# RWKV attention and a two-level expert layer on one core: expert inputs as blocks of 32 tokens by 96 values, transposed by VectorE

## The chip, the cores and the metric

The kernel runs on one core of a Trainium2 chip. All data are 32-bit floats. The metric is the device time of one execution in microseconds (us), as the median of several runs. The profile is one further execution, taken by the hardware profiler. The engines are named as the profile names them: PE is TensorE (matrix multiply), PEld its weight load, DVE is VectorE, ACT is ScalarE, POOL is GpSimd, SP is SyncE, which here only starts transfers. A "q" behind an engine's name is its queue of instructions. Lnnn is a line of the kernel before.

## What is computed

An attention block with a state per head comes first, then a mixture of experts whose expert is chosen in two levels.

```python
B, H, S, D = 4, 8, 768, 48
for t in range(S):
    cur = einsum('bhd,bhe->bhde', u * k[:, :, t], v[:, :, t])
    y[:, :, t] = einsum('bhd,bhde->bhe', r[:, :, t], state + cur)
    state = w[..., None] * state + einsum('bhd,bhe->bhde', k[:, :, t], v[:, :, t])
x = y.transpose(0, 2, 1, 3).reshape(3072, 384)
# N, DM, G, Eg, F = 3072, 384, 4, 4, 1024
g_idx = argmax(x @ w_group);          g_w = softmax(x @ w_group)[g_idx]
e_idx = argmax(x @ w_expert[g_idx]);  e_w = softmax(x @ w_expert[g_idx])[e_idx]
out = g_w * e_w * (relu(x @ w1[g_idx, e_idx]) @ w2[g_idx, e_idx])
```

The term with u (the "own term" of a token) needs only r, k, v of that token: the sum over a head of r u k, times v.

## The kernel before

The attention is computed in 24 tiles of 128 tokens (six pieces of the sequence for each of four batches). A loop of 29 steps works as a pipeline: in step s, tile s is turned (`turn`), tile s-1 is scored, tile s-2 is multiplied with v (`values`), tile s-3 is turned back and its own term is added (`back`), and tiles s-4 and s-5 are routed. Two tiles make a pair, and one pair of r, k, v is one load each. The routed rows of 384 values, with two more for the token number and the gate, are scattered to `x_sorted` in DRAM, by expert. Their places are first filled with zeros there, because a fixed number of slots of each expert is processed, filled or not.

```python
SLOTS = [256, 240, 233, 222, 216, 212, 206, 202, 199, 196, 193, 190, 187, 184, 178, 173]
CAP = max(SLOTS); FOUR = 4
w1f = moe_w1.rearrange("g e (ko p) f -> (g e) p ko f", p=P)
...
nothing = cst([P, XW], "nothing")
...
def zero_places(j):
    regions = xs_dram.rearrange("(e n) w -> n e w", e=GE)
    part = CAP // 4
    nc.scalar.dma_start(out=regions[part * j : part * (j + 1)], in_=spread(nothing[0:part, :], 1, GE))
...
def load_expert(e, i, queue=nc.sync):
    w1, w2 = places[i]
    queue.dma_start(out=w1, in_=w1f[bass.ds(e, 1)].rearrange("a p k f -> (a p) k f"))
    queue.dma_start(out=w2, in_=w2f[bass.ds(e, 1)].rearrange("a p k f -> (a p) k f"))
    return w1, w2
...
ITEMS = [(0, 0, P), (0, P, SLOTS[0])] + [(e, 0, SLOTS[e]) for e in range(1, GE)]

def load_rows(i, expert, queue):                       # L472
    ...
    for j, n in enumerate(parts(i)):
        a = ITEMS[i][1] + P * j
        queue.dma_start(out=xg[0:n, j, :], in_=by_expert[bass.ds(expert, 1), a : a + n, :]...)

def columns(i):
    ...
    for ks in (range(0, KO),) if KO * w <= 512 else (range(0, 2), range(2, KO)):
        px = bank([P, len(ks), w], "px")
        for q, ko in enumerate(ks):
            for j, n in enumerate(parts(i)):
                nc.tensor.transpose(px[:, q, P * j : P * j + n],                # L483
                                    xg[0:n, j, P * ko : P * (ko + 1)], ident[0:n, 0:n])
        nc.vector.tensor_copy(xe[:, ks[0] : ks[-1] + 1, 0:w], px)               # L486
    ...                                                # ids and gates from the two last values of xg

def up(i, f): ...      # L506: w1 times xe into ph; ScalarE: relu into hT
def down(i, d): ...    # L520: w2 times hT into po; ScalarE copies to yo
def rows_out(i): ...   # L530: three transposes a part; VectorE times the gate; scatter to out
...
def own(g):            # GpSimd: dg = r * k * u of pair g
def own_sum(g):        # VectorE: du = sum of dg over a head        (L558)
def own_values(n):     # ScalarE: dv = v * du, one product a head   (L564)
...
for s in range(NT + LAST):
    if s % 2 == 0 and s // 2 + 2 < NP: load_pair(s // 2 + 2)
    if s in (3, 5, 7, 9): zero_places(s // 2 - 1)
    if s == FOUR * B + 7:
        first = expert_of(first_i[0:1, 0:1], (SP,))
        weights[0] = load_expert(first, 0)
    if s == FOUR * B + 9:
        load_rows(0, first, nc.sync)
        second = expert_of(first_i[0:1, 1:2], (SP,))
        weights[1] = load_expert(second, 1)
    if s == FOUR * B + 10: columns(0)
    run("first")
    if s < NT: turn(s); ...                            # and own(s // 2 + 1) in odd steps
    for n in range(NT):
        if s == max(n + 1, 2): own_values(n)
    run("choice")
    ...                                                # rows_T, row_logits, back, values
    if s % 2 == 0 and 0 < s // 2 < NP: own_sum(s // 2)
    run("last")                                        # gates, places, scatters of rows
    if 0 <= s - 1 < NT: scores(s - 1)
    ...
    if s == FOUR * B + 10: up(0, 0)
up(0, 2); up(0, 4); ...; up(0, 6)
load_rows(1, first, nc.sync)
...
down(0, 0); ...; down(0, 1); down(0, 2); rows_out(0)
load_rows(2, second, nc.sync)
columns(1)
for i in range(1, len(ITEMS)):                         # this order is kept on TensorE alone
    up(i, 0); up(i, 2)
    if i > 1: rows_out(i - 1)
    up(i, 4); up(i, 6)
    load_rows(i + 2, expert, nc.sync)
    down(i, 0)
    if i + 1 < len(ITEMS): columns(i + 1)
    down(i, 1); down(i, 2)
    weights[e] = load_expert(expert, e % 2)            # the expert of item i + 2
```

The first 16 tiles decide which two experts come first (`pick_first`), so that item 0, the first 128 slots of the first expert, can be computed while the last tiles are still routed. Two sets of weights are held at a time.

Of the kernel before, what the change touches and what calls it, by code (L numbers as in the profile page):

```python
# [8 lines left out]
FP32 = mybir.dt.float32  # L9
# [6 lines left out]
P = 128  # L16
# [18 lines left out]
def kernel(  # L35
# [40 lines left out]
    w1f = moe_w1.rearrange("g e (ko p) f -> (g e) p ko f", p=P)  # L76
# [12 lines left out]
    def cst(shape, name, dtype=FP32):  # L89
        return const.tile(shape, dtype, name=name)  # L90
# [80 lines left out]
    nothing = cst([P, XW], "nothing")  # L171
# [148 lines left out]

    def zero_places(j):

        regions = xs_dram.rearrange("(e n) w -> n e w", e=GE)
        part = CAP // 4
        nc.scalar.dma_start(out=regions[part * j : part * (j + 1)], in_=spread(nothing[0:part, :], 1, GE))
# [101 lines left out]
    def load_expert(e, i, queue=nc.sync):  # L427

        w1, w2 = places[i]
        queue.dma_start(out=w1, in_=w1f[bass.ds(e, 1)].rearrange("a p k f -> (a p) k f"))  # L430
        queue.dma_start(out=w2, in_=w2f[bass.ds(e, 1)].rearrange("a p k f -> (a p) k f"))
        return w1, w2

    def transposed(x, dst):

        px = bank([P, KO, P], "px")
        for ko in range(KO):
            nc.tensor.transpose(px[:, ko, :], x[:, P * ko : P * (ko + 1)], ident)
        nc.scalar.copy(dst, px)
# [7 lines left out]
    by_expert = xs_dram.rearrange("(e n) w -> e n w", e=GE)  # L447
# [14 lines left out]

    def load_rows(i, expert, queue):
        shape = [P, room(i) // P, XW]
        if i < 3:
            xg = pools[0].tile(shape, FP32, name=f"xg_{i}")
        else:
            xg = pools[1].tile(shape, FP32, tag="xg", bufs=3, name="xg")
        xgs[i] = xg
        for j, n in enumerate(parts(i)):  # L470
            a = ITEMS[i][1] + P * j
            queue.dma_start(  # L472
                out=xg[0:n, j, :], in_=by_expert[bass.ds(expert, 1), a : a + n, :].rearrange("a n w -> (a n) w")
            )

    def columns(i):
        xg, w = xgs.pop(i), width(i)
        xe = xes[i] = item_tile(i, [P, KO, room(i)], "xe")
        for ks in (range(0, KO),) if KO * w <= 512 else (range(0, 2), range(2, KO)):
            px = bank([P, len(ks), w], "px")  # L480
            for q, ko in enumerate(ks):
                for j, n in enumerate(parts(i)):
                    nc.tensor.transpose(  # L483
                        px[:, q, P * j : P * j + n], xg[0:n, j, P * ko : P * (ko + 1)], ident[0:n, 0:n]
                    )
            nc.vector.tensor_copy(xe[:, ks[0] : ks[-1] + 1, 0:w], px)  # L486
        ids = item_tile(i, [P, 2], "ids", U32, bufs=4)
        gates = item_tile(i, [P, 2], "gates", bufs=4)
        for j, n in enumerate(parts(i)):
            nc.vector.tensor_scalar(  # L490
                out=ids[0:n, j : j + 1], in0=xg[0:n, j, DM + ROW_ID : DM + ROW_ID + 1], scalar1=float(N),
                scalar2=None, op0=OP.add,
            )
            nc.vector.tensor_copy(gates[0:n, j : j + 1], xg[0:n, j, DM + ROW_GATE : DM + ROW_GATE + 1])
        keys_of[i] = ids, gates
# [155 lines left out]
    def rows_T(n):  # L651
        xTs[n] = pool.tile([P, KO, P], FP32, tag="xT", bufs=2, name="xT")
        c, b = tiles[n]
        transposed(xts[c][:, b, 0:DM], xTs[n])
# [36 lines left out]
    for s in range(NT + LAST):  # L691
# [15 lines left out]
        if s == FOUR * B + 7:  # L707
            first = expert_of(first_i[0:1, 0:1], (SP,))
            weights[0] = load_expert(first, 0)
        if s == FOUR * B + 9:  # L710
            load_rows(0, first, nc.sync)
            second = expert_of(first_i[0:1, 1:2], (SP,))
            weights[1] = load_expert(second, 1)
# [9 lines left out]
        for n in range(NT):  # L723
            if s == max(n + 1, 2):
                own_values(n)
# [10 lines left out]
        if s % 2 == 0 and 0 < s // 2 < NP:  # L736
            own_sum(s // 2)
        run("last")
        if 0 <= s - 1 < NT:
            scores(s - 1)  # L740
        if s == 1:
            own_sum(0)

# [9 lines left out]
        if n in ROUTED:  # L753
# [8 lines left out]
            else:  # L762
                todo.setdefault(s + 1, []).append(("choice", choice))
                todo.setdefault(s + 2, []).extend([("first", before), ("last", gate), ("last", place)])
                for i in range(T):
                    at = s + 3 + (i // 2 if n == FOUR * B - 1 else i)
                    todo.setdefault(at, []).append(("last", lambda i=i, rows=rows: rows(i)))
# [62 lines left out]
    with tc.If(more > 0, preferred_fallthrough_block=False):  # L830
        with tc.tile_pool(name="rest", bufs=1) as rest:
# [15 lines left out]
            with tc.If(ok < 1):  # L847
                with tc.tile_pool(name="scan", bufs=1) as sc:
# [54 lines left out]
                    with tc.For_i(0, NT, 1) as i:  # L903
# [6 lines left out]
                        transposed(xr[:, 0, 0:DM], xT)  # L910
# [62 lines left out]
            with tc.For_i(0, GE, 1) as i:  # L973
                at = nc.values_load(
                    ends_i[0:1, bass.ds(i, 1)], min_val=0, max_val=GE * RG - P,
                    skip_runtime_bounds_check_because="a region holds all tokens and a slot",
                )
                nc.sync.dma_start(out=xs_dram[bass.ds(at, P), :], in_=nothing)
# [4 lines left out]
            with tc.For_i(0, slots, 1) as i:  # L983
# [14 lines left out]
                )  # L998
                xe = tl([P, KO, P], "xe")
                transposed(xg[:, 0:DM], xe)  # L1000
# [50 lines left out]
```

## Time and profile before

| | |
|---|---|
| median of 3 runs | 480.44 us (475.02 to 482.15) |
| the profiled run, its span | 479.58 us, 477.9 us |
| mean granted clock of TensorE | 0.973 of full |
| busy: PE, PEld, DVE, ACT, POOL | 449.7, 430.6, 159.5, 139.0, 129.5 us |
| data moved by DMA | 86.24 MB in 112024 packets, 79633 of them under 512 B |
| transposes of expert inputs on TensorE (L483) | 96, from 168.1 to 447.5 us |
| copies of them by VectorE (L486) | 32, mean 475 ns |
| weights per expert, w1 and w2 | 1536 KB each, 6.8 to 7.1 us from issue to landing |

A line of a timeline gives the start in us, the duration, the engine, the line and operation, output and inputs with their sizes, and in brackets how long the engine had been idle before it and what released it. "[2.88 <-ACT yT L616]" is: idle for 2.88 us, until ScalarE had written yT in line 616. Matmuls are pipelined, so the time that a group of them holds TensorE is read from one start to the next group's start, not from the durations. A 32-bit product is recorded as two instructions.

### The profile page before, as it was taken

The page shows a single profiled execution, that of the slowest core. Times are in us where ns is not written, and L with a number is a line of the kernel's source. Part 1 is how long each engine was busy: PE and PEld are TensorE (multiplying, and loading weights), DVE is VectorE, ACT ScalarE, POOL GpSimd, SP SyncE. Part 2 cuts the span into 40 slices and gives each one's busy share as a digit, 9 for nine tenths or more (in the row PEclk, how much of TensorE's full clock was granted, in tenths as well). Part 3 has the DMA queues.
Part 4 walks back from the last instruction along what each step waited for, and adds up shares of the span by engine and source line. Part 5 has one row for each costly group of instructions (what it writes and reads, how often), then busy time and mean ns, then how long its engine had stood idle before and what let it go on. Part 6 is the DMA issues. An engine that isn't in the chain of part 4 may idle for free. (4 is left out here: it accounts for less than half of the span.)

```text
span 477.9 us, 9090 instructions
## 1 busy us (share of the span) xinstructions
PE 449.7 (94%) x3623; PEld 430.6 (90%) x3623; DVE 159.5 (33%) x478; ACT 139.0 (29%) x418; POOL 129.5 (27%) x135
## 2 busy tenths in 40 slices
PE   3799999999999898999999999999999999999992
PEld 2598888899999798999999999999999999999991
DVE  5546566877778663010110210110110110111000
ACT  2846553564656321111121111111111111111120
POOL 7834536556564042000010210110120110120011
PEclk9969979999999989999999999999999999999997
DMA  9999999983102994565465754755856765666000
GB/s 176 187 190 228 207 227 202 200 155 77 36 35 69 339 335 132 188 239 168 160 190 182 256 184 153 280 201 156 284 190 198 255 188 199 238 202 236 30 22 26
DMA packets 112024, 86.24 MB, mean 180 GB/s; under 512 B 79633, under 2 KB 103568, under 8 KB 111976
## 3 DMA queue, kind: packets, MB, share of 16 engines
q1 hardware_dynamic: 98920, 68.81, 52.1%
q10 hardware_dynamic: 8432, 7.31, 7.1%
q0 software_dynamic: 4624, 9.48, 5.8%
q8 instruction: 30, 0.49, 0.5%
q14 instruction: 18, 0.15, 0.1%
HBM read 69.79 MB, written 16.12 MB: 180 GB/s over the span
## 5 line engine op out<-in xcount | busy, mean ns | idle before, releaser
L534 POOL DMA_INDIRECT out_dram<-yt,ids x32 | 34.1, 1066 | 255.0 <-DVE yt L532 250.4
L506 PE MATMUL ph<-xe,w 128*128 128x128 f32 (+7 forms) x432 | 72.2, 325 | 0.7 <-DVE xe L486 0.7
L520 PE MATMUL po<-hT,w 128*128 128x128 f32 (+7 forms) x432 | 71.4, 322 | 0.0
L506 PEld LDWEIGHTS ph<-xe,w 128*128 128x128 f32 x432 | 69.0, 194 | 1.2 <-DVE xe L486 0.9
L532 DVE TENSOR_SCALAR yt<-pb,gates 128x384 f32<-128x384 f32 (+15 forms) x32 | 18.3, 611 | 153.4 <-PE pb L530 153.4
L520 PE MATMUL po<-hT,rall 128*128 128x240 f32 (+7 forms) x384 | 68.6, 336 | 0.0
L506 PE MATMUL ph<-xe,kall 128*128 128x240 f32 (+7 forms) x384 | 68.4, 335 | 0.0
L520 PEld LDWEIGHTS po<-hT,w 128*128 128x128 f32 x432 | 67.8, 190 | 0.5
L510 ACT ACTIVATE hT<-ph 128x256 f32<-128x256 f32 (+15 forms) x68 | 33.5, 493 | 112.9 <-PE ph L506 112.9
L520 PEld LDWEIGHTS po<-hT,rall 128*128 128x128 f32 x384 | 65.0, 190 | 0.7
L506 PEld LDWEIGHTS ph<-xe,kall 128*128 128x128 f32 x384 | 64.9, 190 | 0.6
L523 ACT COPY yo<-po 128x128 f32<-128x128 f32 (+15 forms) x51 | 16.3, 320 | 127.7 <-PE po L520 127.7
L564 ACT ACTIVATE dv<-vt,du 128x48 f32<-128x48 f32 x192 | 45.8, 324 | 1.1 <-DVE du L558 1.0
L594 DVE TENSOR_TENSOR am<-pa,later 128x512 f32<-128x512 f32 x48 | 30.9, 685 | 9.0 <-PE pa L589 8.7
L486 DVE COPY xe<-px 128x384 f32<-128x384 f32 (+30 forms) x32 | 14.0, 475 | 53.6 <-PE px L483 53.6
L410 POOL DMA_INDIRECT x_sorted<-xt,place_i x24 | 23.8, 990 | 27.9 <-issue 14.0
L589 PE MATMUL pa<-rT,kT 48*128 48x128 f32 x384 | 29.3, 291 | 0.7 <-DVE xt L646 0.7
L611 PE MATMUL py<-am,vt 128*64 128x128 f32 x384 | 29.2, 290 | 0.7 <-DVE am L594 0.6
L553 POOL TENSOR_TENSOR dg<-rall,kall 128x768 f32<-128x768 f32 x12 | 21.9, 1821 | 28.9 <-DVE du L558 28.9
L548 POOL TENSOR_TENSOR kh<-kall,T 128x768 f32<-128x768 f32 (+1 forms) x12 | 21.4, 1788 | 28.0 <-DMA kall<-in_k_dram 9.7
L611 PEld LDWEIGHTS py<-am,vt 128*64 128x64 f32 x384 | 22.7, 143 | 4.7 <-DVE am L594 1.5
L589 PEld LDWEIGHTS pa<-rT,kT 48*128 48x128 f32 x384 | 24.4, 193 | 2.6 <-DVE xt L646 0.9
(128 smaller groups left out, 469.6 us busy)
## 6 DMA issues: line engine op xcount, KB each, us to landing
w<-in_moe_w_dram SPq DMA_DIRECT2D x16, 1536.0 KB, 6.8
kall<-in_moe_w_dram SPq DMA_DIRECT2D x8, 1536.0 KB, 7.1
rall<-in_moe_w_dram SPq DMA_DIRECT2D x8, 1536.0 KB, 6.8
x_sorted<-nothing ACTq DMA_DIRECT2D x4, 1544.0 KB, 10.2
rall<-in_r_dram SPq DMA_DIRECT2D x12, 384.0 KB, 7.2
vt<-in_v_dram SPq DMA_DIRECT2D x12, 384.0 KB, 6.8
kall<-in_k_dram SPq DMA_DIRECT2D x10, 384.0 KB, 6.4
xg<-x_sorted SPq DMA_DIRECT2D x17, 193.0 KB, 6.2
```

Of the source, the lines that this page charges most:

```text
L410: ins = nc.gpsimd.indirect_dma_start(out=xs_dram, out_offset=bass.IndirectOffsetOnAxis(ap=place_i[:, i : i + 1], axis=0), in_=xt[:, i, :], ...
L506: nc.tensor.matmul(ph[:, q, :], lhsT=w1[:, ko, P * (f + q) : P * (f + q + 1)], rhs=xe[:, ko, 0:w], start=(ko == 0), stop=(ko == KO - 1), s ...
L510: nc.scalar.activation(hTs[i][:, f : f + 2, 0:w], ph, AF.Relu)
L520: nc.tensor.matmul(po, lhsT=w2[:, fo, P * d : P * (d + 1)], rhs=hT[:, fo, 0:w], start=(fo == 0), stop=(fo == FO - 1))
L532: nc.vector.tensor_scalar(out=yt[0:n], in0=pb[0:n], scalar1=gates[0:n, j : j + 1], scalar2=None, op0=OP.mult)
L534: ins = nc.gpsimd.indirect_dma_start(out=out, out_offset=bass.IndirectOffsetOnAxis(ap=ids[0:n, j : j + 1], axis=0), in_=yt[0:n], in_offset ...
L548: engine.tensor_mul(khs[g % (RING - 1)][:, a0:a1, :, 0:D], kts[g % RING][:, a0:a1], spread(T2[m], 1, a1 - a0))
L553: nc.gpsimd.tensor_mul(dg, rts[g % RING][:, :, :, 0:D], kts[g % RING])
L564: nc.scalar.mul(dv[:, h, :], vts[g % (RING + 1)][:, a, h, 0:D], dvs[g][:, a, h : h + 1])
L589: nc.tensor.matmul(pa[e][:, hc, :], lhsT=kT[rows, hc, :], rhs=rT[rows, hc, :], start=True, stop=True, skip_group_check=True,)
L594: nc.vector.tensor_mul(am[:, e], pa[e], spread(later, 1, HP))
L611: nc.tensor.matmul(py[DP * e : DP * (e + 1), hc, :], lhsT=vt[:, a, 2 * hc + e, :], rhs=am[:, e, hc, :], start=(c == 0), stop=True, skip_gr ...
```

## The change

There are four parts.

1. The inputs of an expert are read from `x_sorted` with the token number modulo 32 on the partitions: four transfers, one for each group of 32 partitions, take 96 of the 384 values of every token, for blocks of 32 tokens. VectorE transposes every 32 by 32 block in place of TensorE's 128 by 128 transposes and the copies out of PSUM. Value 96 q + 32 k + d of a token then lies on partition 32 q + d, in column group k; the rows of w1 are loaded in the same order, in four transfers, one for each q. Token number and gate are read apart, as `key`. Numbers of slots are rounded up to 32 in the load and in the transpose.
2. The zero fill writes packets of two rows (3088 bytes) from 128 partitions, for four experts at a time, in place of packets of one row (1544 bytes) from 64 partitions, for all sixteen.
3. The own terms are taken later: `own_values` of a tile one step later (from step n + 2), `own_sum` after the scores.
4. Around the first experts: in step 23 w1 of the first expert, then its rows, then its w2 and the second expert's weights are requested; before, the rows and the second expert came in step 25. The four scatters of the last of the first 16 tiles are issued in one step.

What it is for: TensorE is relieved of the transposes of the expert inputs, the zero fill is to load the DMA engines less, and the own terms are to stand less in the way of the copies and masks that TensorE waits for.

```diff
-    w1f = moe_w1.rearrange("g e (ko p) f -> (g e) p ko f", p=P)
+    BL = 32
+    w1f = moe_w1.rearrange("g e (q ko p) f -> (g e) q p ko f", ko=KO, p=BL)
...
-    nothing = cst([P, XW], "nothing")
+    nothing = cst([P, CAP // P, XW], "nothing")
...
     def zero_places(j):
-        regions = xs_dram.rearrange("(e n) w -> n e w", e=GE)
-        part = CAP // 4
-        nc.scalar.dma_start(out=regions[part * j : part * (j + 1)], in_=spread(nothing[0:part, :], 1, GE))
+        e, a = GE // 4, CAP // P
+        nc.scalar.dma_start(
+            out=regions[e * j : e * (j + 1), 0:CAP, :].rearrange("e (p a) w -> p e (a w)", a=a),
+            in_=spread(nothing.rearrange("p a w -> p (a w)"), 1, e),
+        )
...
+    def load_w1(e, i):
+        for q in range(P // BL):
+            nc.sync.dma_start(
+                out=places[i][0][BL * q : BL * (q + 1)], in_=w1f[bass.ds(e, 1), q].rearrange("a p k f -> (a p) k f")
+            )
...
     def load_rows(i, expert, queue):
...
-        for j, n in enumerate(parts(i)):
-            a = ITEMS[i][1] + P * j
+        n = room(i)
+        xg, key = xgs[i] = tl([P, n // BL, KO, BL], "xg"), tl([P, n // P, ROW_EXTRA], "key")
+        a, w, rows = ITEMS[i][1], padded(width(i)), regions[bass.ds(expert, 1)]
+        for q in range(P // BL):
             queue.dma_start(
-                out=xg[0:n, j, :], in_=by_expert[bass.ds(expert, 1), a : a + n, :].rearrange("a n w -> (a n) w")
-            )
+                out=xg[BL * q : BL * (q + 1), 0 : w // BL].rearrange("t b k d -> t b (k d)"),
+                in_=rows[:, a : a + w, BL * KO * q : BL * KO * (q + 1)].rearrange("a (b t) d -> t (a b) d", t=BL),
+            )
+        n = P * len(parts(i))
+        queue.dma_start(out=key[:, 0 : n // P], in_=rows[:, a : a + n, DM:XW].rearrange("a (j p) w -> p (a j) w", p=P))
 
     def columns(i):
...
-        for ks in (range(0, KO),) if KO * w <= 512 else (range(0, 2), range(2, KO)):
-            px = bank([P, len(ks), w], "px")
...
-            nc.vector.tensor_copy(xe[:, ks[0] : ks[-1] + 1, 0:w], px)
+        for ko in range(KO):
+            nc.vector.transpose(xe[:, ko, 0:w].rearrange("p (b t) -> p b t", t=BL), xg[:, 0 : w // BL, ko, :])
...
         if s == FOUR * B + 7:
             first = expert_of(first_i[0:1, 0:1], (SP,))
-            weights[0] = load_expert(first, 0)
-        if s == FOUR * B + 9:
-            load_rows(0, first, nc.sync)
             second = expert_of(first_i[0:1, 1:2], (SP,))
-            weights[1] = load_expert(second, 1)
+            load_w1(first, 0)
...
-            if s == max(n + 1, 2):
+            if s == n + 2:
                 own_values(n)
...
-        if s % 2 == 0 and 0 < s // 2 < NP:
-            own_sum(s // 2)
         run("last")
+        if s == FOUR * B + 7:
+            load_rows(0, first, nc.sync)
+            load_w2(first, 0)
+            weights[0], weights[1] = places[0], load_expert(second, 1)
         if 0 <= s - 1 < NT:
             scores(s - 1)
         if s == 1:
             own_sum(0)
+        if s % 2 == 0 and 0 < s // 2 < NP:
+            own_sum(s // 2)
...
-                    at = s + 3 + (i // 2 if n == FOUR * B - 1 else i)
+                    at = s + 3 + (0 if n == FOUR * B - 1 else i)
```

The paths for inputs that fit no fixed number of slots are adapted too; they do not run here.

## Prediction

> **What bounds the kernel now.** I read the page first, then the windows by stage, then the timeline of TensorE, with the waits beside it. The columns of a window are: stretch, then busy time (and instructions) of PE, PEld, DVE, ACT and POOL, the granted TensorE clock, the DMA share and GB/s.
>
> ```profile
> PE 449.7 (94%) x3623; PEld 430.6 (90%) x3623; DVE 159.5 (33%) x478; ACT 139.0 (29%) x418; POOL 129.5 (27%) x135
> ...
> 24.00:32.00 8.00, 8.00 (x65) 7.35 (x63) 3.30 (x8) 3.53 (x13) 2.93 (x4) 0.50 1.17 186
> ...
> 165.00:168.00 3.00, 0.09 (x1) 0.00 (x0) 1.76 (x9) 1.21 (x4) 0.00 (x0) 1.00 0.94 273
> ...
> 240.00:260.00 20.00, 20.00 (x114) 19.91 (x113) 2.39 (x8) 3.55 (x8) 1.96 (x2) 1.00 0.55 190
> ```
>
> So there are three stages. From about 200 us to the end (experts), TensorE has no gap at full clock, and DVE (2.39 of 20) and the DMA engines (0.55) have room. Up to about 100 us the DMA share is 1.0 or more and the clock at times half. Between them, near 165 and 186 us, TensorE stands still for x_sorted. The 94% alone would hide the second and third point. The chain of work that ended last has only four pieces here, from 470 us on, and says nothing of the rest; so I go by gaps and by starts in order.
>
> In the expert stage, what counts is the time from one start to the next on TensorE (start, duration, instruction):
>
> ```profile
> 212.65 0.77 PE L483 MATMUL px<-ident,xg 128*128 128x128 f32 x6
> 213.26 6.66 PE L520 MATMUL po<-hT,rall 128*128 128x240 f32 x32
> ...
> 429.71 1.36 PE L483 MATMUL px<-ident,xg 128*128 128x128 f32 x6
> 431.01 5.25 PE L520 MATMUL po<-hT,rall 128*128 128x184 f32 x32
> ```
>
> The six transposes of one item hold TensorE 0.61 us, and 1.30 us in the last five items, where the second part has 62 rows or fewer. The stops between the stages:
>
> ```profile
> 168.09 0.52 PE L483 MATMUL px<-ident,xg 128*128 128x128 f32 x3 [3.00 <-DMA xg<-x_sorted]
> ...
> 186.72 0.52 PE L483 MATMUL px<-ident,xg 128*128 128x128 f32 x3 [0.69 <-DMA xg<-x_sorted]
> 187.89 5.62 PE L506 MATMUL ph<-xe,w 128*128 128x128 f32 x48 [0.65 <-DVE xe L486]
> ```
>
> And the one large stop of the first stage, with the loads behind the zero fill:
>
> ```profile
> 21.24 0.95 DVE L558 TENSOR_REDUCE du<-dg 128x16 f32<-128x768 f32 x1 [2.58 <-POOL dg L554]
> 21.70 0.66 PE L645 MATMUL pb<-ident,yT 128*128 128x128 f32 x4 [2.88 <-ACT yT L616]
> 22.97 2.35 PE L611 MATMUL py<-am,vt 128*64 128x128 f32 x15 [0.61 <-DVE am L594]
> ...
> 36.79 8.29 SPq L133 DMA_DIRECT2D vt<-in_v_dram  x1
> ...
> x_sorted<-nothing ACTq DMA_DIRECT2D x4, 1544.0 KB, 10.2
> ```
>
> TensorE waits 2.88 us for yT, which ScalarE copies only after sixteen own-term products; then for am, which stands on VectorE behind a du that itself waited 2.58 us for GpSimd. The load of v sits 8.29 us in its queue while the zero fill of 35.38 us runs.
>
> [...]clock 0.50 from 24 to 32 us after the 2.88 us stop, and 0.50 from 170 to 172 after the 3.00 us one. [...]a pair of tiles of r, k, v (6144 packets of 192 B, 384 per engine) passes in 5.5 us at best (loads of 71.20 to 76.72), 14 ns a packet and 13 GB/s an engine, while the weights near 160 us ran at 377 GB/s, 24 an engine.
>
> **The change part by part.**
>
> *Expert transposes.* Removed from TensorE: 96 transposes. For items 2 to 16 the start-to-start sums are 0.63, 0.61, 0.59, 0.57, 0.56, 0.55, 0.54, 0.53, 0.52, 0.51 and 1.33, 1.32, 1.31, 1.30, 1.28: 12.15 us, all on the engine that bounds this stage. Added to VectorE: three block transposes per item, for two PSUM copies of 475 ns mean. [...] They are placed after the first third of the down product; the other two thirds take over 5 us on TensorE (213.26 to 219.76 at 240 columns), so xe is ready. Gain 12.2.
>
> *Weights and rows.* w1 goes in four transfers to 32 partitions[...] against 4.2 at 377 GB/s. w2 stays at 4.2. Rows: 1024 packets of 384 B and 256 of 8 B for 256 of 1544 B; at 25 ns a packet (estimate, between the 14 ns seen at 192 B and the 65 ns of 1544 B at 24 GB/s) 64 per engine make 1.6 us, the keys 0.2. [...] against item periods of 20.35 us (199.35 to 219.76) at first and 452.62 - 436.10 - 1.28 = 15.2 at the end. w1 is asked for when the up product two items earlier is over and needed one and a half periods later, over 22 us, so I expect no wait[...].
>
> *From routing to experts.* Step 23 now loads w1, then the first rows, then w2 and the second expert; the last four scatters of the first 16 tiles are issued together, and compete with 1.5 MB instead of 3. The rows were issued at 163.12; I expect about 160, landed by 165. VectorE is in routing until 166.97, so xe is ready near 168.1. TensorE no longer stops at the transposes: it goes on with 2.0 us of work (168.45 to 170.49) from 165.1 to 167.1, waits about 1 us and keeps its clock; the up products until 179.74 took 9.25 us, of which about 1.1 was half clock. Down starts near 176.2, 3.5 us earlier. The last scatter comes as much earlier, at 177.8, its landing at 180.7 (before 181.32 and 184.23). But the next rows are now four transfers that leave about 0.57 us apart: last issued 182.4, landed 185 (2.4 to 2.8 us were the shortest seen), three transposes, restart near 186.2 instead of 187.89. TensorE is then idle from 182.5 to 186.2, enough to lose the clock, which costs up to 2 us. Net: about 0, between +3 and -3.
>
> *Own terms later.* ScalarE has eight products (1.91 us) ahead of yT instead of sixteen, so pb can start near 20.0 instead of 21.70; am no longer stands behind du. Step 3, 17.73 to 28.31 = 10.58 us, should take about 5.3, and step 4 at full clock 5.2 instead of 7.00: 7.1 us. Part is lost again: the k of pair 3 was issued at 28.27, lands some 6.4 us later and is scaled in 1.82 us, which is 36.5, when step 6 would want it near 34. Keep 4.5.
>
> *Zero fill.* The ACT queue's 7.1% of 477.9 us is 33.9 us; less about 3.9 for the first two k and u, four fills take 7.5 us of all engines each. Half as many packets, out of 128 partitions instead of 64, at the weights' rate: 4.2 us. So 13 us of DMA time go from the first 65 us. TensorE gains only what it waited for: steps 9, 10, 11 and 13 run 1.7, 3.0, 1.1 and 1.3 us over the steady 6.07 (102.18 to 150.76 in eight steps), partly a half clock whose cause I can't name. I take half, 3.5.
>
> **Sum.** 12.2 + 0 + 4.5 + 3.5 = 20.2 us; 480.4 - 20.2 = 460.
>
> **Rivals.** *First: the weight transfers become the bound.* [...] Against: a DMA share of only 0.55 to 0.70 now[...]. If w1 came at 130 GB/s (12 us), an item would need 19 us, and the late ones would wait 2 to 4 us each: about 475 to 485. *Second: the rows after routing come later.* For it: five transfers in place of one ahead of each transpose. If xe of item 1 comes at 190, TensorE idle 7 us and cold, the handover loses 5: about 465. *Third: the first stage is bound by DMA anyway.* For it: a share above 1 until 100 us; steps then begin earlier only to wait for pair 3 and 4, the 8 us vanish: 468. Against: from 76.72 on a pair takes the queue about 6 us and TensorE 12. *Fourth, upward:* no half clock before 100 us at all. The six slow steps exceed 6.07 by 12.4 us together: 455.
>
> **Range and chances.** The 12.2 us are read off the bounding engine, plus or minus 1 unless transfers bind; the first stage is 8 plus or minus 5, the handover 0 plus or minus 3, and the three runs before spread over 7 us. 8 times in 10 between 450 and 470. Two per cent is 470.8, which needs the first stage to yield nothing and something else to be lost: faster 0.88, within 0.09, slower 0.03.
>
> **What would show it.** Right: windows after 200 us with TensorE at 20.00 and a period shorter by 0.5 to 1.3 us per item; [...] step 3 near 5 us with no clock of 0.50 around 24 to 32; zero fill landing well under 10 us; a gap near 182 on a transfer or on xe. Wrong: waits of ph on w1 or of po on w2 in the late items; DVE transposes of over 1 us; a half clock at the same places. If the expert stage did not shorten by about 12 us, the reading of the bound is wrong; if only the first stage failed to shorten, the transfers rule it.

## The result, and the profile after

The changed kernel takes 461.24 us (median of 4 runs, 460.36 to 463.68). The kernel before, on the same chip, takes 479.49 us (475.02 to 482.15). The ratio is 0.9657, with a 95% interval from 0.9575 to 0.974. The prediction was 460, in a range from 450 to 470.

The total agrees, but the sum behind it does not hold term by term. I divide both profiled executions (477.9 and 458.6 us) at two instructions that both have: the first product of step 23 on TensorE, and the first up product of item 2.

| stretch (us) | before | after | difference | predicted |
|---|---|---|---|---|
| start to step 23 (attention, routing) | 150.76 | 138.68 | -12.1 | -8.0 |
| step 23 to item 2 (handover) | 48.59 | 53.86 | +5.3 | 0 |
| item 2 to the end (experts) | 278.55 | 266.06 | -12.5 | -12.2 |
| span | 477.9 | 458.6 | -19.3 | -20.2 |

The expert stage is right. The first stage gave 4 us more than predicted, and the handover took 5 us back. In the lines that follow, line numbers are those of the kernel that is named.

The page of the changed kernel, first the busy times of the engines, then two queues (packets, MB, share of the time of 16 DMA engines); q1 is SyncE's, q10 ScalarE's, which carries the zero fill:

```profile
PE 429.4 (94%) x3527; PEld 416.0 (91%) x3527; DVE 156.7 (34%) x497; ACT 138.8 (30%) x418; POOL 129.9 (28%) x135
...
q1 hardware_dynamic: 115532, 69.19, 66.3%
...
q10 hardware_dynamic: 6384, 7.31, 4.8%
```

TensorE has 96 instructions and 20.3 us of busy time less, and its share is 94% again: the kernel is shorter, and the same engine is the busiest. Queue q10 took 33.9 us of all DMA engines before and takes 22.0 now (4.8% of 458.6).

Windows of the changed kernel; the columns are those of the prediction (busy times with instructions, granted clock, DMA share, GB/s):

```profile
24.00:32.00 8.00, 8.00 (x102) 7.41 (x102) 6.59 (x15) 6.10 (x21) 4.47 (x5) 1.00 1.18 195
156.00:162.00 6.00, 5.59 (x27) 5.60 (x27) 3.23 (x18) 1.69 (x6) 3.88 (x4) 0.50 1.07 334
174.00:180.00 6.00, 0.80 (x6) 0.37 (x4) 0.68 (x2) 0.27 (x1) 0.97 (x1) 0.99 0.33 78
240.00:260.00 20.00, 20.00 (x112) 19.96 (x112) 2.26 (x9) 3.17 (x8) 2.54 (x3) 1.00 0.78 195
400.00:420.00 20.00, 20.00 (x132) 19.98 (x132) 2.15 (x9) 3.47 (x9) 2.65 (x2) 1.00 0.95 227
```

From 24 to 32 us TensorE starts 102 instructions at full clock where it started 65 at half. The handover now holds 6 us at half clock and 5 us in which TensorE does nothing. In the expert stage TensorE is still busy all the time, and the DMA engines, which were at 0.55 from 240 to 260 us, are at 0.78 there and at 0.95 later.

The stop at the start of step 3, in the timeline of the changed kernel (start, duration, engine, instruction, idle before and releaser):

```profile
18.03 0.66 PE L593 MATMUL pr<-ident,rall 128*128 128x128 f32 x4
18.82 1.29 DVE L612 TENSOR_TENSOR am<-pa,later 128x512 f32<-128x512 f32 x2
...
20.03 0.66 PE L663 MATMUL pb<-ident,yT 128*128 128x128 f32 x4 [0.91 <-ACT yT L634]
...
24.08 0.66 PE L593 MATMUL pr<-ident,rall 128*128 128x128 f32 x4
```

The wait for yT is 0.91 us instead of 2.88; the mask am starts at 18.82 instead of 22.22, because no du stands before it. The step, from pr to pr, takes 6.05 us instead of 10.58.

The handover, in the timeline of the changed kernel:

```profile
151.22 1.88 SPq L493 DMA_DIRECT2D xg<-x_sorted  x4
...
154.09 1.90 ACT L582 ACTIVATE dv<-vt,du 128x48 f32<-128x48 f32 x8
...
156.41 1.47 PE L458 MATMUL rb<-gw,xT 128*128 128x20 f32 x6 [1.45 <-ACT xT L454]
...
170.47 0.97 POOL L417 DMA_INDIRECT x_sorted<-xt,place_i  x1 [0.30 <-issue]
...
176.15 1.86 SPq L493 DMA_DIRECT2D xg<-x_sorted  x4
...
179.94 0.70 DVE L505 STREAM_TRANSPOSE xe<-xg 128x128 f32<-128x128 f32 x3 [4.34 <-DMA xg<-x_sorted]
...
180.39 6.95 PE L524 MATMUL ph<-xe,w 128*128 128x128 f32 x48 [5.45 <-DVE xe L505]
```

TensorE no longer stops for the transposes of the first rows. It stops 1.45 us for xT, because ScalarE first does the eight own-term products of the last tile, and the half clock follows. Then the last scatter is issued at 170.47, the next rows are requested only 5.68 us later, and TensorE is idle for 5.45 us. The 48 up products after that take 6.95 us instead of 5.62, again partly at half clock (mean 0.77 from 180 to 187 us).

The same pair of instructions in the kernel before, first for the rows of item 0 and then for those of item 1:

```profile
155.19 0.97 POOL L410 DMA_INDIRECT x_sorted<-xt,place_i  x1 [0.30 <-issue]
...
163.12 0.35 SPq L472 DMA_DIRECT2D xg<-x_sorted  x1
...
181.32 0.97 POOL L410 DMA_INDIRECT x_sorted<-xt,place_i  x1 [0.30 <-issue]
...
184.23 2.96 SPq L472 DMA_DIRECT2D xg<-x_sorted  x5
```

For item 1 it takes 2.91 us. For item 0, with the 3 MB of the first expert's weights on the DMA engines (share 0.99 from 156 to 162 us), it takes 7.93 us. So the profile before already showed both a short and a long delay.

### The profile page after: what moved, and what is told of

Its sections match the earlier page's. It is cut to its first block, busy times and chain, and to the rows that moved or that the text cites. A ratio compares the mean times of both kernels' runs of the same rounds, so it can differ in the third digit from the quotient of the medians.

```text
span 458.6 us, 9289 instructions
## 1 busy us (share of the span) xinstructions
PE 429.4 (94%) x3527; PEld 416.0 (91%) x3527; DVE 156.7 (34%) x497; ACT 138.8 (30%) x418; POOL 129.9 (28%) x135
## 3 DMA queue, kind: packets, MB, share of 16 engines
q1 hardware_dynamic: 115532, 69.19, 66.3%
## 5 line engine op out<-in xcount | busy, mean ns | idle before, releaser
L524 PE MATMUL ph<-xe,w 128*128 128x128 f32 (+7 forms) x432 | 73.9, 330 | 5.5 <-DVE xe L505 5.5
L524 PEld LDWEIGHTS ph<-xe,w 128*128 128x128 f32 x432 | 70.6, 199 | 5.9 <-issue 5.6
L538 PE MATMUL po<-hT,w 128*128 128x128 f32 (+7 forms) x432 | 69.6, 321 | 0.0
L538 PE MATMUL po<-hT,rall 128*128 128x240 f32 (+7 forms) x384 | 67.0, 334 | 0.0
L629 PE MATMUL py<-am,vt 128*64 128x128 f32 x384 | 26.5, 279 | 0.0
L566 POOL TENSOR_TENSOR kh<-kall,T 128x768 f32<-128x768 f32 (+1 forms) x12 | 21.4, 1789 | 14.2 <-DMA kall<-in_k_dram 12.2
L597 ACT COPY kT<-pk 128x512 f32<-128x512 f32 x24 | 14.0, 583 | 33.7 <-PE pk L593 32.4
L629 PEld LDWEIGHTS py<-am,vt 128*64 128x64 f32 x384 | 20.7, 136 | 3.1 <-issue 0.7
```

Of the source, the lines that this page charges most:

```text
L524: nc.tensor.matmul(ph[:, q, :], lhsT=w1[:, ko, P * (f + q) : P * (f + q + 1)], rhs=xe[:, ko, 0:w], start=(ko == 0), stop=(ko == KO - 1), s ...
L538: nc.tensor.matmul(po, lhsT=w2[:, fo, P * d : P * (d + 1)], rhs=hT[:, fo, 0:w], start=(fo == 0), stop=(fo == FO - 1))
L566: engine.tensor_mul(khs[g % (RING - 1)][:, a0:a1, :, 0:D], kts[g % RING][:, a0:a1], spread(T2[m], 1, a1 - a0))
L629: nc.tensor.matmul(py[DP * e : DP * (e + 1), hc, :], lhsT=vt[:, a, 2 * hc + e, :], rhs=am[:, e, hc, :], start=(c == 0), stop=True, skip_gr ...
```

## The experiments

Four stretches of the profiled execution say more than a total. "Down" is the first down product of item 0, "item 1" and "item 2" their first up products; the last column is from the issue of the last scatter of routed rows to the request of the rows of item 1.

| kernel | median | step 23 starts | to up of item 0 | to down | to item 1 | to item 2 | item 2 to end | scatter to request |
|---|---|---|---|---|---|---|---|---|
| before | 480.1 | 150.76 | 19.73 | 9.25 | 8.15 | 11.46 | 278.55 | 2.91 |
| own_alone | 473.84 | 144.34 | 18.93 | 9.33 | 8.28 | 11.47 | 278.45 | 3.01 |
| zero_alone | 474.00 | 142.12 | 21.10 | 13.69 | 8.02 | 11.46 | 278.51 | 2.97 |
| own_and_zero | 467.34 | 139.57 | 19.46 | 9.73 | 8.17 | 11.46 | 278.51 | 2.84 |
| dve_alone | 473.02 | 150.74 | 20.60 | 14.07 | 8.07 | 12.42 | 266.10 | 2.84 |
| early_loads | 470.63 | 140.17 | 18.55 | 12.95 | 7.87 | 11.46 | 278.50 | 2.83 |
| after | 461.24 | 138.68 | 19.91 | 10.06 | 11.74 | 12.15 | 266.06 | 5.68 |
| after_again | 461.16 | 138.77 | 18.93 | 9.71 | 12.42 | 13.46 | 266.11 | 6.23 |
| dv_early | 460.88 | 138.88 | 19.27 | 10.93 | 11.97 | 12.23 | 266.12 | 6.75 |
| whole_w1 | 457.06 | 138.63 | 19.56 | 9.99 | 9.41 | 10.80 | 266.11 | 3.76 |
| late_and_dv | 455.62 | 138.74 | 17.70 | 10.93 | 8.91 | 10.80 | 266.12 | 3.36 |
| two_queues | 455.29 | 138.68 | 17.35 | 9.81 | 8.95 | 12.42 | 266.09 | 3.26 |
| two_and_warm | 454.64 | 138.70 | 17.43 | 9.87 | 8.98 | 10.80 | 266.12 | 3.14 |

The kernel before took 480.13, 480.05 and 479.95 us beside the three sets of four runs.

### One part of the change alone

**own_alone**: part 3 in the kernel before.

```diff
-            if s == max(n + 1, 2):
+            if s == n + 2:
                 own_values(n)
...
-        if s % 2 == 0 and 0 < s // 2 < NP: own_sum(s // 2)      # ahead of run("last")
+        if s % 2 == 0 and 0 < s // 2 < NP: own_sum(s // 2)      # behind the scores
```

> The kernel before, with part 3 of the change alone: own_values of a tile one step later, own_sum after the scores. The changed kernel starts tile 23 (step 23) 12.1 us earlier than the kernel before (138.68 after 150.76), and its steps 3 and 4 are 6.5 us shorter. Theory A (the own terms alone cause the stop at 18 to 22 us and the half clock behind it): the gap of 2.88 us before the product pb at yT is below 1.2 us, step 3 takes about 6 instead of 10.6 us, step 23 starts about 6 us earlier, and the whole is 5 to 7 us shorter. Theory B (what counts is the load of pair 3 behind the zero fill, as the prediction's 2.6 us taken back say): step 3 is shorter, but steps 5 or 6 wait for k of pair 3, and step 23 starts at most 4 us earlier.

Measured: 473.84 us, ratio 0.989 (0.9866 to 0.9914). Step 23 starts 6.4 us earlier, step 3 takes 4.79 us. That is theory A in size, but theory B's loss is there too. In its timeline:

```profile
28.45 1.84 SPq L133 DMA_DIRECT2D kall<-in_k_dram  x1
...
34.94 1.81 POOL L548 TENSOR_TENSOR kh<-kall,T 128x768 f32<-128x768 f32 x1 [7.65 <-DMA kall<-in_k_dram]
...
36.80 0.66 PE L575 MATMUL pk<-ident,kh 128*128 128x128 f32 x4 [1.11 <-POOL kh L548]
...
44.67 0.66 PE L575 MATMUL pr<-ident,rall 128*128 128x128 f32 x4
```

The k of pair 3 is requested at 28.45 us, lands some 6.5 us later, and TensorE waits for it in step 6, which takes 9.64 us (35.03 to 44.67) instead of 6.45. The clock, 1.00 until 36 us, is 0.85 and 0.72 in the 8 us after. So 3.2 us are lost, as the prediction had it (2.6).

**zero_alone**: part 2 in the kernel before.

```diff
-        part = CAP // 4
-        nc.scalar.dma_start(out=regions[part * j : part * (j + 1)], in_=spread(nothing[0:part, :], 1, GE))
+        e, a = GE // 4, CAP // P
+        nc.scalar.dma_start(out=regions[e * j : e * (j + 1), 0:CAP, :].rearrange("e (p a) w -> p e (a w)", a=a),
+                            in_=spread(nothing.rearrange("p a w -> p (a w)"), 1, e))
```

> The kernel before, with part 2 alone: zero fill in packets of 3088 bytes from 128 partitions. Theory A (zero fill matters only for what TensorE waits for later, steps 9 to 13): step 3 stays near 10.6 us with its stop of about 2.9 us; steps 9 to 11 together take 19 to 21 us instead of 23.9; the whole is 3 to 5 us shorter. Theory B (the first stage is led by the DMA engines): step 23 starts 6 us or more earlier. Theory C (the zero fill lies beside other work): no more than 1.5 us.

Measured: 474.00 us, ratio 0.988 (0.985 to 0.991). Step 23 starts 8.6 us earlier: theory B's size. Steps 9 to 11 take 19.43 us instead of 23.91, as theory A has it. What it did not have is steps 3 and 4, 12.60 instead of 17.58 us. The stop is still there in its timeline, but shorter:

```profile
22.00 0.66 PE L649 MATMUL pb<-ident,yT 128*128 128x128 f32 x4 [1.79 <-ACT yT L620]
```

It ends as late as before (22.00, 21.70), but TensorE comes to it later, as step 3 starts 1.4 us later. The clock stays at 1.00 after 1.79 us, where it fell to 0.50 after 2.88. So 5 of the 8.6 us lie in two steps whose stop this time did not cost the clock. The median gains 6.1 us, less than the 8.6: in the profiled execution the handover has 17 us of half clock (158 to 175), and the way from up to down takes 13.69 us.

**own_and_zero**: both of these edits.

> The kernel before, with parts 2 and 3, the experts as before. If parts 2 and 3 explain the whole of the first stage, step 23 starts near 138.7 us as in the changed kernel, 12 us earlier, and the whole is about 468 us. If they add up, this run's gain is the sum of the gains of the two runs with one part; if part 3 needs part 2 (pair 3's k comes late without it), it is more than the sum by about 2.6 us.

Measured: 467.34 us, ratio 0.9753 (0.97 to 0.9807). The two gains in the median, 6.3 and 6.1, make 12.4; measured are 12.8. At step 23 the gains, 6.4 and 8.6, make 15.0; measured are 11.2, because both take away the same half clock of steps 3 and 4, and each alone already shortens steps 9 to 11 (19.73 us in own_alone, 19.43 in zero_alone, 18.58 with both, 23.91 before). Against that, the loss in step 6 is gone (step 6 takes 6.45 us). Step 23 starts at 139.57, 0.9 us later than in the changed kernel: parts 2 and 3 explain the first stage.

**dve_alone**: part 1 in the kernel before, with the loads of steps 23 and 25 as before.

```diff
-            nc.vector.tensor_copy(xe[:, ks[0] : ks[-1] + 1, 0:w], px)        # after the transposes on TensorE
+        for ko in range(KO):
+            nc.vector.transpose(xe[:, ko, 0:w].rearrange("p (b t) -> p b t", t=BL), xg[:, 0 : w // BL, ko, :])
```

> The kernel before, with part 1 alone: blocks of 32 by 32 turned by VectorE, w1 in four transfers to 32 partitions; zero fill, own terms and the order of the loads around step 23 as before. Theory A (the transposes held TensorE, which is the bound of the expert stage): from the first product of item 2 to the end 12 to 12.5 us less than before (278.55), no gap of TensorE after item 2, whole 467 to 470 us, with a handover that costs 0 to 2 us. Theory B (the handover's 5.3 us come from part 1 itself, that is from the small transfers of the rows and four-part w1): the stretch from step 23 to item 2 is 4 us or more longer than the 48.6 us of before, whole 471 to 474 us.

Measured: 473.02 us, ratio 0.9851 (0.9784 to 0.9918). From item 2 to the end 266.10 us, 12.4 less: theory A's mechanism, and no other part touches that stretch. The handover is 55.16 us, 6.6 more, as theory B has it. But not where theory B looks for it: the rows of item 1 are requested 2.84 us after the last scatter, and item 1 follows down after 8.07 us, both as before. What is long is the way from up to down. Its timeline, then a window:

```profile
170.92 0.70 DVE L503 STREAM_TRANSPOSE xe<-xg 128x128 f32<-128x128 f32 x3 [3.97 <-DMA xg<-x_sorted]
...
171.34 2.90 PE L522 MATMUL ph<-xe,w 128*128 128x128 f32 x12 [4.28 <-issue]
```

```profile
176.00:180.00 4.00, 4.00 (x19) 4.00 (x20) 2.16 (x12) 0.00 (x0) 2.19 (x3) 0.50 1.06 347
```

The first up products come 0.42 us after the first block is turned, so the "issue" is a wait for xe. TensorE stood still for 4.28 us, and the clock is 0.50 until about 184 us.

### What the handover waits for

**early_loads**: parts 2, 3 and 4, without part 1.

```diff
         if s == FOUR * B + 7:
-            weights[0] = load_expert(first, 0)          # rows and the second expert two steps later
+            second = expert_of(first_i[0:1, 1:2], (SP,))
+            nc.sync.dma_start(out=places[0][0], in_=w1f[bass.ds(first, 1)].rearrange("a p k f -> (a p) k f"))
...
         run("last")
+        if s == FOUR * B + 7:
+            load_rows(0, first, nc.sync)
+            nc.sync.dma_start(out=places[0][1], in_=w2f[bass.ds(first, 1)].rearrange("a p k f -> (a p) k f"))
+            weights[0], weights[1] = places[0], load_expert(second, 1)
```

> The kernel before, with parts 2, 3 and 4 and without part 1: expert inputs still turned by TensorE, w1 still one transfer, but the loads ordered as in the changed kernel. With parts 2 and 3 alone the stretch from the start of step 23 to the first product of item 2 was 48.8 us, in the changed kernel 53.9 to 54.5. Theory A (part 1's small transfers and four-part w1 cost the handover, part 4 gives some of it back): the stretch is 45 to 48 us, the whole 464 to 467 us. Theory B (requesting both sets of weights behind the first rows costs the handover, whatever the transposes): the stretch is 52 us or more, the whole 470 us or more, and the rows of item 1 are requested 5 us or more after the last scatter was issued.

Measured: 470.63 us, ratio 0.9789 (0.9724 to 0.9853), and 50.83 us from step 23 to item 2, which lies between the two theories; neither holds. Against theory B, the rows follow the last scatter after 2.83 us:

```profile
172.97 0.97 POOL L414 DMA_INDIRECT x_sorted<-xt,place_i  x1 [0.30 <-issue]
...
175.80 2.96 SPq L476 DMA_DIRECT2D xg<-x_sorted  x5
```

The DMA share, 1.07 from 166 to 168 us, is 0.27 by then. Against theory A, what part 4 gave (the up products come 0.91 us sooner after step 23 than in own_and_zero) was lost again: the clock is 0.50 from 160 to 168 us, after a wait of 1.46 us for xT, and up to down takes 12.95 us. So neither in dve_alone (part 1 without part 4) nor here (part 4 without part 1) are the rows of item 1 late. But in both, half clock had held back the last scatter, to 35.97 and 32.80 us after the start of step 23 instead of 31.79, when the weights were in; that it takes both parts is not shown by these two runs alone.

**whole_w1**: the changed kernel with w1 in one transfer to 128 partitions. Its rows are then in the old order, which the inputs no longer have, so the products pair w1 with the wrong inputs; number and size of all operations stay.

```diff
-        for q in range(P // BL):
-            nc.sync.dma_start(
-                out=places[i][0][BL * q : BL * (q + 1)], in_=w1f[bass.ds(e, 1), q].rearrange("a p k f -> (a p) k f"))
+        nc.sync.dma_start(out=places[i][0], in_=w1f[bass.ds(e, 1)].rearrange("a p k f -> (a p) k f"))
```

> The changed kernel, but w1 is loaded in one transfer to 128 partitions, its rows in the order of before. They don't fit the order of the inputs then, so the sums over w1 pair the wrong values; number and size of all operations stay. Theory A ([...]w1 takes twice as long): w1 lands in about 4.5 us instead of 8 or more, the DMA share after 300 us falls by about 0.2, the expert stage stays at 266.1 us because TensorE bounds it, the handover becomes 0 to 2 us shorter: 459 to 461 us. Theory B (four quarters together fill the DMA engines): no change of the share, same time.

Measured: 457.06 us (456.08 to 458.51; ratio to the kernel before 0.9534, 0.948 to 0.9588), 4.1 us less than after_again (461.0 to 462.47), more than theory A had. The expert stage stays at 266.11 us. In its timeline, and in two windows, the second one with nothing but a w1 under way:

```profile
169.88 0.97 POOL L417 DMA_INDIRECT x_sorted<-xt,place_i  x1 [0.30 <-issue]
...
173.64 1.89 SPq L490 DMA_DIRECT2D xg<-x_sorted  x4
...
177.59 2.58 PE L521 MATMUL ph<-xe,w 128*128 128x128 f32 x21 [3.12 <-DVE xe L502]
```

```profile
400.00:420.00 20.00, 20.00 (x135) 19.97 (x134) 3.88 (x14) 3.78 (x9) 3.46 (x3) 1.00 0.79 259
294.00:297.00 3.00, 3.00 (x20) 3.00 (x19) 0.00 (x0) 0.33 (x1) 0.00 (x0) 1.00 1.02 422
```

The changed kernel, also with nothing but a w1 under way:

```profile
298.00:304.00 6.00, 6.00 (x36) 6.00 (x36) 0.00 (x0) 0.66 (x2) 0.00 (x0) 1.00 1.05 210
```

The wide transfer moves 422 GB/s, the four quarters 210, with the DMA engines busy in both (share 1.02 and 1.05). So theory A has the size, half the rate, and theory B is right only in that the four quarters fill the DMA engines too. From 400 to 420 us the share falls from 0.95 to 0.79.

The rows are requested 3.76 us after the scatter instead of 5.68 to 6.23. Between 172 and 174 us the DMA share is 0.03 here and 0.97 in the changed kernel; there it falls to 0.06 at 174, and the rows are requested at 176.15. The last scatter is issued 31.25 us after the start of step 23, no later than in the changed kernel (31.79), so this time it is not a late scatter that makes the delay short. So the four-part w1 of part 1 makes the block of weights behind the first rows (part 4) last longer, and the last scatters lie in it.

The queue of SyncE has 57.3% of 454.5 us here and 66.3% of 458.6 in the changed kernel: 260.4 and 304.1 us of all engines. The 43.7 us over 16 transfers make 2.7 us a w1 that the narrow destination costs, with no wait of TensorE for it outside the handover (item 2 to the end: 266.11 and 266.06 us).

**late_w2, dv_early, late_and_dv**: the changed kernel, with w2 of the second expert requested after the rows of item 2, with the last own product in step 24 instead of 25, and with both.

```diff
-            weights[0], weights[1] = places[0], load_expert(second, 1)
+            weights[0], weights[1] = places[0], places[1]
+            load_w1(second, 1)
...
     load_rows(2, second, nc.sync)
+    load_w2(second, 1)
```

```diff
-            if s == n + 2:
+            if s == min(n + 2, NT):
                 own_values(n)
```

> The changed kernel, but w2 of the second expert is requested after the rows of item 2, 1.5 MB less behind the first rows. Theory A (w2 of the first and both weights of the second expert, 4.7 MB, keep the DMA engines busy while the last scatters run, so the rows of item 1 are requested late): the rows of item 1 are requested 2 to 3 us sooner after the last scatter's issue than in the changed kernel (5.7 us), item 1 starts near 177.5 instead of 180.39, whole 2 to 3 us shorter. Theory B (the five small transfers and their transposes make the delay): the rows are requested no sooner than 5 us after the last scatter, whole within 1 us of the changed kernel.

> The changed kernel, but own_values of the last tile is taken one step earlier, in step 24, where ScalarE is idle for over 4 us. Theory A (those 1.9 us of ScalarE ahead of the copy of xT make TensorE wait 1.45 us near 156 us, and the half clock from 156 to 162 us follows from it): that wait goes below 0.5 us, no clock of 0.50 between 156 and 162 us, the first down product starts 2 to 3 us earlier, whole 1 to 3 us shorter. Theory B (the wait only moves to the transfers behind it): whole within 1 us.

> Both edits of the two runs before it in one kernel. If the handover's two causes are apart, their gains add: 3 to 5 us shorter than the changed kernel, 456 to 458 us. If both only wait for the same transfers, it is no shorter than the better of the two.

> The changed kernel itself, for the comparison on the same chip: 461 us within 1 per cent.

Measured: late_w2 456.67 us (454.81 to 463.5; ratio 0.9515, 0.9445 to 0.9584), dv_early 460.88 (460.03 to 463.23), late_and_dv 455.62 (454.89 to 457.96; ratio 0.9521, 0.9448 to 0.9595), after_again 461.16. The profiled execution of late_w2 was its slow one, 463.5 us with a lower mean clock, so it has no row in the table, and the other four are compared (median 456.27, up to 456.68). They are 4.9 us shorter than after_again, more than theory A had. In its profile the rows are requested 2.84 us after the last scatter; that alone can't test theory A, but late_and_dv, below, does.

dv_early is theory B. The wait for xT near 156 us is gone; one of 0.82 us comes at 162 us with half clock behind it, and the rows are requested 6.75 us after the scatter, 5.68 in the changed kernel.

late_and_dv takes 5.5 us off. Its timeline:

```profile
168.67 0.98 POOL L417 DMA_INDIRECT x_sorted<-xt,place_i  x1 [0.30 <-issue]
...
172.03 1.85 SPq L493 DMA_DIRECT2D xg<-x_sorted  x4
...
176.28 5.60 PE L524 MATMUL ph<-xe,w 128*128 128x128 f32 x48 [2.62 <-DVE xe L505]
```

The request follows after 3.36 us, though the last scatter is issued earlier (29.93 us after the start of step 23) than in the changed kernel; this is theory A. The gap of TensorE is 2.62 us instead of 5.45, the 48 products take 5.60 us at full clock, and the whole handover is 48.34 us, as long as before the change. Whether dv_early adds anything to late_w2 (0.65 us between the medians) can't be said: their ranges overlap.

**two_queues, two_and_warm**: late_and_dv with two of the four row transfers of item 1 on ScalarE's queue; and with four idle transposes besides.

```diff
+    down(0, 1)
+    rest_of[1](expert_of(first_i[0:1, 0:1], (mybir.EngineType.Activation,)), nc.scalar)   # row groups 2 and 3
     down(0, 2)
...
+        if s in (FOUR * B + 10, FOUR * B + 11):
+            for q in range(2): nc.tensor.transpose(pw[:, q], ident, ident)
```

> The kernel of the run with both edits (455.6 us), and two of the four row transfers of item 1 are requested by ScalarE's queue instead of SyncE's. Theory A (what is left of the gap before item 1, 2.62 us, is the five requests one after the other, 0.57 us apart): the gap becomes about 1.6 us, the whole 454 to 455 us. Theory B (it is the landing of the last scatter and of the rows): within 0.5 us of 455.6.

> The kernel of two_queues with four more transposes of the identity on TensorE, two ahead of the first up products and two in the next step, whose results nobody reads. Theory A (the half clock from 161 to 165 us follows from several short waits of TensorE just ahead of it, 2.2 us in 10): the clock stays at 1.00 there and the whole is 1 to 2 us shorter, near 453 us. Theory B (the filled time is too short to matter, or it delays the work behind it as much as it gains): within 0.5 us of two_queues.

Measured: 455.29 us (454.19 to 455.57; ratio 0.9484, 0.9434 to 0.9534) and 454.64 us (453.44 to 456.55), which can't be told apart from each other or from late_and_dv. In two_queues the gap before item 1 is 1.60 us, as theory A expects. But ScalarE, which now waits with the request, copies yo later, and TensorE waits 1.20 us for that; down to item 1 stays at 8.95 us. Theory B holds for the time. The idle transposes can't be judged: already in two_queues the clock is 1.00 from 160 to 168 us. One window of each, two_queues and then two_and_warm:

```profile
176.00:180.00 4.00, 4.00 (x24) 4.00 (x23) 1.43 (x7) 0.77 (x2) 0.00 (x0) 0.57 0.88 259
```

```profile
176.00:180.00 4.00, 4.00 (x39) 4.00 (x38) 1.43 (x7) 1.15 (x3) 0.00 (x0) 1.00 0.88 252
```

TensorE was idle for 1.20 and 1.60 us ahead of it in the first, for 1.08 and 1.76 us in the second. One has the half clock, which costs 1.6 us in that item (12.42 and 10.80), and the other hasn't.

## Why the prediction was right in its sum and wrong in two terms

**The expert stage was right.** "12.2 us" came out as 12.5, and dve_alone has it by itself (12.4). Each of items 2 to 10 is 0.56 to 0.63 us shorter, and each of items 11 to 15 1.39 to 1.44, the latter 0.1 more than read off. "I expect no wait" is right: TensorE has 20.00 of 20 us from 240 and from 400 us. There is little room left at the end, as the DMA engines have 0.95 of an item of 15.6 us (402.67 to 418.29), which is 14.8 us. What w1 in four parts would cost was not shown by the profile before. It is 2.7 us more a w1 than in one transfer (whole_w1): the four quarters moved 210 GB/s, the wide transfer 422. Nor did that profile show a block transpose of VectorE; it takes 0.33 us for 224 columns (three in 0.98 us). The first item period is 20.41 us, not 20.35; nothing rests on that.

**The first stage: "Keep 4.5" and "I take half, 3.5" were mis-sized.** Taking out the stop of steps 3 and 4 was expected to give 7.1 us and gave 6.5 (17.58 to 11.04). The step that failed is "Part is lost again: the k of pair 3 was issued at 28.27". The time was taken from the profile before, with the old zero fill ahead of it. With part 3 alone it is so, and costs 3.2 us; with part 2 the k is requested at 24.58 us and nobody waits. The zero fill freed 11.9 us of DMA time, as predicted (13), and steps 9 to 11 gave 5.3 us (23.91 to 18.58), not 3.5 over four steps. But these are not the zero fill's own: part 3 alone takes the steps to 19.73 us. The kernel before has half clock in part of the time from 65 to 75 us (mean 0.66) and the others have none there; dve_alone, whose first stage is that of the kernel before, has it from 54 to 61 us instead, in a step 8 of 11.74 us. How much of the 5.3 us is either part's work and how much is chance stays open. The two parts were added as if apart, although one removes the obstacle of the other. The fourth rival, "no half clock before 100 us at all", is what happened (mean clock 1.00 from 0 to 100 us).

**The handover: "Net: about 0" failed, at +5.3.** By the table: +0.2 to the up products, +0.8 to down, +3.6 to item 1, +0.7 to item 2. Three steps of it failed.

- "I expect about 160" for the first rows. They come 12.54 us after the start of step 23, and 12.36 us before the change. Their scatters are issued 0.9 us earlier in the step, but w1 in four parts is ahead of their landing: with w1 in one transfer the rows come after 10.65 us (whole_w1) and 10.44 us (early_loads).
- "waits about 1 us and keeps its clock". The wait for xe went, the wait of 1.45 us for xT, behind the own-term products that part 3 had moved, came in its place, and the clock did fall. Down came 1.0 us later after step 23, not 3.5 us earlier. I had looked at part 3 only where it relieves ScalarE. The wait alone is not all of it: dv_early, without it, has another one with half clock behind it, and down no sooner (30.20 us after the start of step 23, 29.97 in the changed kernel).
- "its landing at 180.7". I carried over the 2.9 us from scatter to request. They hold in six kernels (2.83 to 3.01 us; the DMA share behind the scatter was 0.36 before, from 181 to 184 us, and 0.27 in early_loads), and become 5.68 to 6.75 where the scatters lie behind 4.7 MB of weights, w1 with narrow destinations. The 7.93 us of the first rows in the profile before were the warning. This is the largest term. Either cure, a wide w1 or 1.5 MB less behind the first rows, takes 4.1 or 4.9 us off the whole; the request follows after 3.76 us in whole_w1 and after 3.36 in late_and_dv.

The second rival named this loss ("the handover loses 5: about 465") but gave the five small transfers as the cause. dve_alone has the five transfers and a normal 8.07 us from down to item 1. They may have a share (the gap before item 1 is 1.78 us in dve_alone and 2.62 in late_and_dv, where there was 0.69 and 0.65), but not the main one.

The first rival, weights as the bound, and the third, DMA as the bound of the first stage, are both excluded by the runs. That the losses of the second and the gains of the fourth rival came together, and cancelled, is why the sum was right. That is luck: the handover missed its own range of plus or minus 3 us.

**What stays open.** Whether a given short stop costs the clock, and with it the share of chance in the first stage. And part 4 alone on top of parts 2 and 3 (early_loads against own_and_zero) seems to cost 3.3 us; the two were timed in different sets, their ranges (467.58 to 471.5, 466.44 to 468.62) overlap, and most of the difference in the profiles is half clock.

## What to carry to other kernels

Latencies read from a profile, such as 2.9 us from a scatter to the next request, were seen to hold only for the load of the DMA engines at that place (5.68 us behind 4.7 MB of weights): when loads are moved forward, look at which small, urgent transfers will now lie behind them. Two parts that relieve the same stop or the same queue aren't added (here 15.0 us at step 23 as a sum, 11.2 measured); take the second one's gain from the profile as it would stand after the first. And moving work out of the way on an engine can put it in the way elsewhere, as here for 1.45 us ahead of xT: look at the last tile as well as at the first.

## What the runs showed of the hardware that was not expected

- Whether a short stop brings the half clock could not be told from its length. Stops of 2.88 and 2.35 us near 20 us brought it, one of 1.79 us did not. Near 156 us, stops of 1.45 us, with one of 0.39 us shortly before, brought it. late_and_dv and two_queues, which are the same program up to there, both have stops of 0.39, 0.32 or 0.33 and 0.81 us between 154 and 160 us: the first then has half clock from about 161 to 165 us, the second none. Nor is its length fixed: with TensorE busy, it lasted about 6 us in the changed kernel, 13 in dve_alone and 15 in zero_alone.
- VectorE turned 32-bit blocks at 0.23 us for 128 columns and 0.37 for 256 (three in 0.70 and 1.10 us). A straight line through the two gives, as an estimate, 0.13 us for 128 columns and 0.10 us that does not depend on them.
- A request that waits for a scatter's landing came about 2 us after the DMA engines had drained (174 and 176.15 us in the changed kernel, 172 and 173.64 us in whole_w1), not 2.9 us after the scatter.
